# One decode kernel's loads re-planned: 3 MB slots at fixed places, more of the cache kept on chip, program order on every engine

**Chip, cores, metric.** One core of one Trainium2 chip. The metric is device time in microseconds (us), median of several executions; a profile of one execution gives the span, some 1 to 2 us shorter than the time.

## The reference

One token goes twice through attention over a window of 4,096 cached positions and a gated FFN. Cut to what matters:

```python
x = x + _A_ref(_layernorm(x), A_k_cache, A_v_cache, A_wq, A_wo)   # 32 heads, Dh 192, last 4096 positions
x = x + _B_ref(_layernorm(x), B_w1, B_w3, B_w2)                   # D 640, F 1536
x = x + _A_ref(_layernorm(x), A_k_cache, A_v_cache, A_wq, A_wo)   # the same caches and weights again
x = x + _B_ref(_layernorm(x), B_w1, B_w3, B_w2)
```

Every byte of K, V and the weights is used for one token only, so the work is reading: a head's K or V is 1.57 MB, 64 of them a layer. What layer 1 still finds on chip from layer 0 it need not read. wq and wo are the weights before and after the attention; w1, w3 and w2 are those of the FFN.

## The kernel before

A ring of five 1.5 MB pages serves all loads; K of eleven heads stays in tiles of its own. VectorE (DVE) transposes each K page, TensorE (PE) forms scores and weighted sums.

```python
NRING = 5
RETAIN = (0, 1, 2, 8, 9, 10, 16, 17, 18, 24, 25)
...
def k_page(layer, h, s_ps):
    if layer == 0 or h not in RETAIN:
        x = ...                                # a retained tile or a ring page
        nc.sync.dma_start(out=x[:], in_=A_k_cache[0, h, S0:SK, :].rearrange("(p t) d -> p (t d)", p=P))
        ...                                    # two DVE transposes
    for it in range(6):
        be, par = divmod(it, 2)
        for th in range(2):
            nc.tensor.matmul(s_ps[32 * th:32 * th + 32, :], lhsT=wst[:, hl, it, :],
                             rhs=_ap(x[:], 0, P, 3072 * th + 64 * be + par, [[192, 16], [2, 32]]), ...)
...
for layer in range(2):
    attention(layer)      # wq, K and V of 4 blocks of 8 heads, then all of wo
    layernorm()
    ffn(...)
```

Of the kernel before, what the change touches and what calls it, by code (L numbers as in the profile page):

```python
# [13 lines left out]
PSUM = bass.MemoryType.PSUM  # L14

# [9 lines left out]
PGW = 6144  # L25
# [3 lines left out]
NRING = 5  # L29
RETAIN = (0, 1, 2, 8, 9, 10, 16, 17, 18, 24, 25)  # L30
KSPLIT = 2
# [8 lines left out]
def kernel(  # L40
# [16 lines left out]

    cst = ctx.enter_context(tc.tile_pool(name="cst", bufs=1))
    wrk = ctx.enter_context(tc.tile_pool(name="wrk", bufs=1))
    sml = ctx.enter_context(tc.tile_pool(name="sml", bufs=2))  # L60
    ring = ctx.enter_context(tc.tile_pool(name="ring", bufs=NRING))
    xrp = ctx.enter_context(tc.tile_pool(name="xrp", bufs=1))
    ps_s = ctx.enter_context(tc.tile_pool(name="ps_s", bufs=2, space=PSUM))
    ps_a = ctx.enter_context(tc.tile_pool(name="ps_a", bufs=4, space=PSUM))
    ps_m = ctx.enter_context(tc.tile_pool(name="ps_m", bufs=2, space=PSUM))

    nc.scalar.preload_act_table_set("natural_log_exp_and_others")

    xb = cst.tile([P, NCH], BF16, name="xb")
    nc.sync.dma_start(out=xb[:], in_=A_x[0, 0, :].rearrange("(p c) -> p c", c=NCH))  # L70

    onesD = cst.tile([P, P], F32, name="onesD")
# [9 lines left out]

    sel4 = cst.tile([P, 4], BF16, name="sel4")
    nc.gpsimd.memset(sel4[:], 0.0)
    nc.gpsimd.affine_select(out=sel4[:], in_=sel4[:], compare_op=ALU.not_equal, fill=1.0, base=0,
                            pattern=[[-32, 4]], channel_multiplier=1)
    sel16 = cst.tile([P, 4, 4], BF16, name="sel16")
    nc.gpsimd.memset(sel16[:], 0.0)
    nc.gpsimd.affine_select(out=sel16[:], in_=sel16[:], compare_op=ALU.not_equal, fill=1.0, base=0,
                            pattern=[[-32, 4], [-1, 4]], channel_multiplier=1)  # L90
    selp = cst.tile([P, 2, HB], BF16, name="selp")
    nc.gpsimd.memset(selp[:], 0.0)
    for j in range(4):
        nc.gpsimd.affine_select(out=selp[:], in_=selp[:], compare_op=ALU.not_equal, fill=1.0, base=-(32 * j + 14),
                                pattern=[[-1, 2], [2, HB]], channel_multiplier=1)
    dmask = cst.tile([64, HB], F32, name="dmask")
    nc.gpsimd.memset(dmask[:], 0.0)
    for blk in range(8):
        nc.gpsimd.affine_select(out=dmask[:], in_=dmask[:], compare_op=ALU.not_equal, fill=float(D), base=-(8 * blk + 7),
                                pattern=[[1, HB]], channel_multiplier=1)  # L100
    t0 = cst.tile([64, 32], F32, name="t0")
    nc.gpsimd.memset(t0[:], 0.0)
    tb = cst.tile([64, 32], F32, name="tb")
    nc.gpsimd.memset(tb[:], 0.0)

    wst = cst.tile([P, HB, 6, 32], BF16, name="wst")
    ptm = cst.tile([P, 16 * 144], BF16, name="ptm")
    otd = cst.tile([P, 48], BF16, name="otd")
    otp = cst.tile([P, 8, 32], BF16, name="otp")
    htd = cst.tile([P, 12], BF16, name="htd")  # L110
    htp = cst.tile([P, 8, 32], BF16, name="htp")

    qt_sb = cst.tile([P, 2, 6, 16], BF16, name="qt_sb")
    retained = {}

    def layernorm():
        nc.vector.tensor_tensor(out=xsq[:, 6:6 + NCH], in0=xsq[:, 0:NCH], in1=xsq[:, 0:NCH], op=ALU.mult)
        st_ps = ps_m.tile([P, 12], F32, tag="m", name="st_ps")
        nc.tensor.matmul(st_ps[:], lhsT=onesD[:], rhs=xsq[:], start=True, stop=True)
# [13 lines left out]
    def y_to_residual(y_ps, dst=None):  # L133
        y_sb = wrk.tile([P, D], BF16, tag="w20", name="y_sb")
        nc.scalar.copy(out=y_sb[:, 0:320], in_=y_ps[0][:, 0:320])
        nc.vector.tensor_copy(out=y_sb[:, 320:640], in_=y_ps[1][:, 0:320])  # L136
        yt_ps = ps_m.tile([P, NCH], F32, tag="m", name="yt_ps")
        for c in range(NCH):
            nc.tensor.matmul(yt_ps[:, c:c + 1], lhsT=y_sb[:, c:D:NCH], rhs=onesb[:], start=True, stop=True)
        nc.vector.tensor_tensor(out=(xsq[:, 0:NCH] if dst is None else dst), in0=xsq[:, 0:NCH], in1=yt_ps[:], op=ALU.add)  # L140

    wq_v = A_wq.rearrange("(p c) n -> c p n", c=NCH)

    def qproj():
        q_ps = ps_a.tile([P, 512], F32, tag="a", name="q_ps")
        for c in range(NCH):
            pg = ring.tile([P, PGW], BF16, tag="pg", name="wq_pg")
            nc.sync.dma_start(out=pg[:], in_=wq_v[c])
            for c2 in range(4):
                for j in range(4):  # L150
                    hp = 4 * j + c2
                    nc.tensor.matmul(q_ps[32 * j:32 * j + 32, 0:384], lhsT=xs4[:, c, c2, :],  # L152
                                     rhs=pg[:, 384 * hp:384 * hp + 384],
                                     start=(c == 0 and c2 == 0), stop=(c == NCH - 1 and c2 == 3),
                                     tile_position=(0, 32 * j))
        q_rep = [wrk.tile([P, 6, 4, 32], BF16, tag=("w20", "w21")[par], name=f"q_rep{par}") for par in range(2)]
        for par in range(2):
            src = _ap(q_ps[:], 0, P, par, [[64, 6], [0, 4], [2, 32]])
            if par == 0:
                nc.scalar.copy(out=q_rep[par][:], in_=src)  # L160
            else:
                nc.vector.tensor_copy(out=q_rep[par][:], in_=src)  # L162
        qt_ps = ps_m.tile([P, 2, 6, 16], F32, tag="m", name="qt_ps")
        for hh in range(2):
            for it in range(6):
                be, par = divmod(it, 2)
                nc.tensor.matmul(qt_ps[:, hh, it, :],
                                 lhsT=q_rep[par][:, 3 * hh + be, :, :].rearrange("p a k -> p (a k)"),
                                 rhs=sel16[:].rearrange("p j c -> p (j c)"), start=True, stop=True)
        nc.vector.tensor_copy(out=qt_sb[:], in_=qt_ps[:])  # L170

    def build_w(b):
        for a in range(4):
            dst = _ap(wst[:], 32 * a, 32, 8 * a + 7, [[382, 4], [191, 2], [32, 6]])
            src = _ap(qt_sb[:], 32 * a, 32, 4 * b, [[1, 4], [96, 2], [16, 6]])
            if a % 2 == 1:
                nc.scalar.copy(out=dst, in_=src)  # L177
            else:
                nc.gpsimd.tensor_copy(out=dst, in_=src)  # L179

    def k_page(layer, h, s_ps):
        hl = h % HB
        if layer == 0 or h not in RETAIN:
            if h in RETAIN:
                x = xrp.tile([P, PGW], BF16, tag=f"xr{h}", name=f"xr{h}")
                retained[h] = x
            else:
                x = ring.tile([P, PGW], BF16, tag="pg", name="k_pg")
            nc.sync.dma_start(out=x[:], in_=A_k_cache[0, h, S0:SK, :].rearrange("(p t) d -> p (t d)", p=P))
            w = PGW // KSPLIT  # L190
            for sp in range(KSPLIT):
                nc.vector.transpose(x[:, w * sp:w * (sp + 1)].bitcast(U32), x[:, w * sp:w * (sp + 1)].bitcast(U32))  # L192
        else:
            x = retained[h]
        for it in range(6):
            be, par = divmod(it, 2)
            for th in range(2):
                nc.tensor.matmul(s_ps[32 * th:32 * th + 32, :], lhsT=wst[:, hl, it, :],  # L198
                                 rhs=_ap(x[:], 0, P, 3072 * th + 64 * be + par, [[192, 16], [2, 32]]),
                                 start=(hl == 0 and it == 0), stop=(hl == HB - 1 and it == 5),  # L200
                                 tile_position=(0, 32 * th))

    def softmax_chain(s_ps):
# [3 lines left out]
        r2 = sml.tile([32, 2, HB], F32, tag="r2", name="r2")  # L207
        for th in range(2):
            nc.vector.reduce_max(out=r2[:, th, :], in_=_ap(t1[:], 32 * th, 32, 0, [[1, HB], [8, 4]]), axis=AX.X)
        m8 = sml.tile([32, HB], F32, tag="m8", name="m8")  # L210
        nc.vector.reduce_max(out=m8[:], in_=_ap(r2[:], 0, 32, 0, [[1, HB], [HB, 2]]), axis=AX.X)
        mb = _ap(m8[:], 0, 32, 0, [[0, 4], [1, HB]])
        nc.vector.tensor_scalar_mul(out=tb[0:32, :].rearrange("p (a z) -> p a z", a=4), in0=mb, scalar1=-SCALE)
        nc.scalar.mul(out=tb[32:64, :].rearrange("p (a z) -> p a z", a=4), in_=mb, mul=-SCALE)
        nbt = sml.tile([64, 32], F32, tag="nbt", name="nbt")
        nc.vector.transpose(nbt[:], tb[:])
        e = wrk.tile([64, 512], BF16, tag="w20", name="e")
        l = sml.tile([64, 1], F32, tag="l", name="l")
        nc.scalar.activation(out=e[:], in_=s_ps[0:64, :], func=ACTF.Exp, bias=nbt[:, 0:1], scale=SCALE, accum_out=l[:])  # L219
        et = wrk.tile([64, 512], BF16, tag="w21", name="et")  # L220
        nc.vector.transpose(et[:], e[:])  # L221
        engs = [nc.scalar, nc.vector, nc.scalar, nc.vector, nc.scalar, nc.vector, nc.scalar, nc.scalar]
        for th in range(2):
# [31 lines left out]
    def combine(b, o_ps, rl):  # L255
# [14 lines left out]
        if b == 0:  # L270
            nc.gpsimd.tensor_copy(out=otp[:, 0:4, 0], in_=otd[:, 0:4])
# [85 lines left out]
    def attention(layer):  # L357
# [8 lines left out]
        for k in range(HB):  # L366
            k_page(layer, k, s_ps)
# [51 lines left out]
```

## Time and profile before

| | before |
|---|---|
| time, median of 13 runs | 552.07 us (551.77 to 552.55) |
| span of the profiled run | 550.8 us |
| bytes read | 227.29 MB |
| busy: PE, DVE, ACT | 54%, 41%, 8% of the span |

The page cuts the span into 40 slices: a digit is a busy share in tenths, and a second line gives GB/s. A timeline line has start, duration, engine, source line, operation, operands, count, and in brackets the idle time before it with what ended it. A matmul that waited for a DMA therefore dates a landing, which is the moment at which a transfer's data may be used. The lines are shown in the prediction.

### The profile page before, as it was taken

The numbers are of one execution on the slowest core, as the hardware profiler recorded it, in microseconds if no ns is written. First come the engines' busy times: TensorE is split into PE (matmuls) and PEld (weight loads), VectorE is DVE, ScalarE is ACT, GpSimd is POOL, SyncE is SP. The second block draws the span as 40 slices with busy tenths as digits, with TensorE's granted clock in tenths as the row PEclk, the third lists the DMA queues.
The fourth block names the chain that finished last, engine by engine and source line by source line (L and its number), as shares of the span: only waits on it lengthen the run. The fifth ranks groups of instructions, "written<-read, shape, count | busy, mean of one in ns | idle before, by whom it ended". The sixth has DMA issues, their size and how long they took to land.

```text
span 550.8 us, 5786 instructions
## 1 busy us (share of the span) xinstructions
PE 298.8 (54%) x2448; PEld 124.2 (23%) x2448; DVE 226.5 (41%) x270; ACT 41.9 (8%) x107; POOL 12.2 (2%) x52
## 2 busy tenths in 40 slices
PE   2355555647555556644455386457555765553543
PEld 1111122213222222221222132222222322221221
DVE  2189844374444744420012095444344444420011
ACT  1100200030002000020001002001100300020000
POOL 2000000000000000000000000000000000000000
PEclk9999776576676666565556579776877767565556
DMA  8999999999999999999999999999999999999992
GB/s 342 428 423 427 427 425 427 423 424 424 427 426 426 428 425 426 422 426 418 408 420 427 423 417 428 426 425 426 423 426 427 425 427 425 427 423 419 406 420 94
DMA packets 24618, 227.66 MB, mean 413 GB/s; under 512 B 2704, under 2 KB 2704, under 8 KB 7824
## 3 DMA queue, kind: packets, MB, share of 16 engines
q1 hardware_dynamic: 24592, 227.29, 98.4%
q8 instruction: 19, 0.31, 0.2%
q14 instruction: 7, 0.06, 0.0%
HBM read 227.28 MB, written 0.00 MB: 413 GB/s over the span
## 4 chain that ended last, share of the span: by engine, by line
DMA 73%; PE 16%; DVE 7%; ACT 2%; issue 1%; SPq 0%; DVEq 0%; ACTq 0%
DMA k_pg<-in_A_k_cache_dram 42%; PE s_ps L198 9%; DMA wo_pg<-in_A_wo_dram 9%; DMA v_pg<-in_A_v_cache_dram 8%; DVE k_pg L192 6%; PE o_ps L249 5%; DMA wq_pg<-in_A_wq_dram 5%; DMA fd_pg<-in_B_w_dram 5%; DMA xr<-in_A_k_cache_dram 4%; ACT ptm L229 1%; PE y_ps L292 1%; DVE xr L192 1%; PE q_ps L152 1%; PE y_ps L352 0%; ACT e L219 0%
## 5 line engine op out<-in xcount | busy, mean ns | idle before, releaser
L192 DVE STREAM_TRANSPOSE k_pg<-k_pg 128x1536 uint32<-128x1536 uint32 x84 | 144.2, 1756 | 131.7 <-DMA k_pg<-in_A_k_cache_dram 60.3
L198 PE MATMUL s_ps<-k_pg,wst 128*32 128x512 bf16 x504 | 115.9, 543 | 119.8 <-DVE k_pg L192 119.8
L249 PE MATMUL o_ps<-v_pg,ptm 128*16 128x384 bf16 (+1 forms) x1024 | 133.7, 472 | 28.4 <-DMA v_pg<-in_A_v_cache_dram 23.6
L198 PEld LDWEIGHTS <-wst 128*32 128x32 bf16 x768 | 54.9, 116 | 240.4 <-issue 190.5
L198 PE MATMUL s_ps<-xr,wst 128*32 128x512 bf16 x264 | 53.0, 509 | 26.5 <-DVE xr L192 22.9
L249 PEld LDWEIGHTS <-ptm 128*16 128x16 bf16 (+1 forms) x1024 | 49.9, 109 | 72.6 <-issue 57.8
L192 DVE STREAM_TRANSPOSE xr<-xr 128x1536 uint32<-128x1536 uint32 x22 | 37.7, 1753 | 8.7 <-DMA xr<-in_A_k_cache_dram 8.6
L152 PE MATMUL q_ps<-wq_pg,xs 128*32 128x384 bf16 x160 | 14.7, 518 | 21.4 <-DMA wq_pg<-in_A_wq_dram 20.0
L177 ACT COPY wst<-qt_sb 32x48 bf16<-32x48 bf16 x16 | 6.4, 397 | 237.7 <-PE s_ps L198 233.6
L267 DVE TENSOR_TENSOR otd<-ot_ps,rl 64x12 bf16<-64x12 f32 x16 | 2.9, 184 | 51.0 <-PE ot_ps L262 25.5
L292 PE MATMUL y_ps<-wo_pg,otd 128*1 128x320 bf16 x160 | 15.6, 464 | 14.7 <-DMA wo_pg<-in_A_wo_dram 14.7
L136 DVE CAST y_sb<-y_ps 128x320 bf16<-128x320 f32 x4 | 2.0, 492 | 42.4 <-PE y_ps L292 35.2
L229 ACT COPY ptm<-et 32x128 bf16<-32x128 bf16 x40 | 16.2, 404 | 6.6 <-DVE et L221 6.2
L162 DVE CAST q_rep<-q_ps 128x768 bf16<-128x768 f32 x2 | 1.9, 958 | 35.3 <-ACT q_rep L160 35.3
L257 ACT CAST o_sb<-o_ps 128x384 bf16<-128x384 f32 x8 | 3.8, 478 | 148.3 <-PE o_ps L249 148.3
L179 POOL COPY wst<-qt_sb 32x48 bf16<-32x48 bf16 x16 | 6.2, 385 | 320.6 <-PE s_ps L198 243.6
L204 DVE TENSOR_REDUCE t<-s_ps 64x1 f32<-64x512 f32 x8 | 5.4, 678 | 18.5 <-PE s_ps L198 18.5
L152 PEld LDWEIGHTS <-xs 128*32 128x32 bf16 x160 | 6.2, 130 | 28.7 <-issue 22.3
L292 PEld LDWEIGHTS <-otd 128*1 128x1 bf16 x160 | 6.0, 111 | 23.8 <-issue 19.6
L221 DVE STREAM_TRANSPOSE et<-e 64x512 bf16<-64x512 bf16 x8 | 5.6, 703 | 4.6 <-ACT e L219 4.6
L235 PE MATMUL rl_ps<-ld,onesD 64*128 64x8 f32 x16 | 3.7, 302 | 5.9 <-POOL ld L233 5.9
L231 DVE COPY ptm<-et 32x128 bf16<-32x128 bf16 x24 | 6.2, 260 | 0.5
(79 smaller groups left out, 89.8 us busy)
## 6 DMA issues: line engine op xcount, KB each, us to landing
v_pg<-in_A_v_cache_dram SPq DMA_DIRECT2D x64, 1536.0 KB, 13.4
k_pg<-in_A_k_cache_dram SPq DMA_DIRECT2D x42, 1536.0 KB, 15.2
xr<-in_A_k_cache_dram SPq DMA_DIRECT2D x11, 1536.0 KB, 22.3
wq_pg<-in_A_wq_dram SPq DMA_DIRECT2D x10, 1536.0 KB, 14.0
wo_pg<-in_A_wo_dram SPq DMA_DIRECT2D x10, 1440.0 KB, 16.7
fd_pg<-in_B_w_dram SPq DMA_DIRECT2D x4, 960.0 KB, 12.5
fa_pg<-in_B_w_dram SPq DMA_DIRECT2D x2, 1536.0 KB, 14.3
fb_pg<-in_B_w_dram SPq DMA_DIRECT2D x2, 1536.0 KB, 14.5
```

Of the source, the lines that this page charges most:

```text
L152: nc.tensor.matmul(q_ps[32 * j:32 * j + 32, 0:384], lhsT=xs4[:, c, c2, :], rhs=pg[:, 384 * hp:384 * hp + 384], start=(c == 0 and c2 == 0), ...
L177: nc.scalar.copy(out=dst, in_=src)
L179: nc.gpsimd.tensor_copy(out=dst, in_=src)
L192: nc.vector.transpose(x[:, w * sp:w * (sp + 1)].bitcast(U32), x[:, w * sp:w * (sp + 1)].bitcast(U32))
L198: nc.tensor.matmul(s_ps[32 * th:32 * th + 32, :], lhsT=wst[:, hl, it, :], rhs=_ap(x[:], 0, P, 3072 * th + 64 * be + par, [[192, 16], [2, 3 ...
L204: nc.vector.reduce_max(out=t0[:, 0:1], in_=s_ps[0:64, :], axis=AX.X)
L221: nc.vector.transpose(et[:], e[:])
L229: eng.copy(out=dst, in_=src)
L231: eng.tensor_copy(out=dst, in_=src)
L249: nc.tensor.matmul(o_ps[32 * j:32 * j + mw, 0:384], lhsT=ptm[:, po:po + mw], rhs=vn[:, 384 * u:384 * u + 384], start=(hl == 0 and mq == 0) ...
L257: nc.scalar.copy(out=o_sb[:], in_=o_ps[:, 0:384])
L292: nc.tensor.matmul(y_ps[nh][32 * j:32 * j + mw, 0:320], lhsT=lhsT, rhs=pg[:, 640 * cc + 320 * nh:640 * cc + 320 * nh + 320], start=(ci < 4 ...
```

## The change

The intent: read fewer bytes, in longer rows, and let no part of the chip make the queue of transfers wait. A row, or run, is one contiguous piece of DRAM that goes to one partition. The core of the change, with cuts marked:

```diff
-NRING = 5
-RETAIN = (0, 1, 2, 8, 9, 10, 16, 17, 18, 24, 25)
+SLOT = 64 * DH                 # two heads, 24,576 B per partition
+NSLOT = 7                      # fixed places in one large tile, beside a small ring for weights
+CUT_Q0 = (2, 2, 1)             # how a weight is cut into transfers
 ...
+    ctx.enter_context(tc.manual_schedule(engines={ENG.SP, ENG.PE, ENG.DVE, ENG.Activation, ENG.Pool}))
 ...
+    def need(key):             # issues the planned transfers in order, up to this one
 ...
+            nc.sync.dma_start(out=pg[:, at:at + n], in_=src)
 ...
+    def kv_src(cache, b, z, t0=0, nt=TP):
 ...
+        return bass.AP(cache.tensor, cache.offset + off, [[TP * DH, 64], [SK * DH, 2], [1, nt * DH]])
 ...                            # the plan: every transfer with its place
+                                     rhs=_ap(x, 0, P, 192 * th + 64 * be + par + 2 * h, [[384, 32], [4, 16]]),
 ...
+        order = (0, 1, 2, 3) if layer == 0 else (3, 2, 1, 0)     # layer 1 starts with the retained block
+        for z in range(NZ):
+            if layer == 1 and z < 2:
+                q_rows((range(0, 3), range(3, 5))[z])
+            k_stage(order[0], z, s_ps, z == 0, z == NZ - 1)
 ...                            # wo is read and used block by block, inside the attention loop
+    def ffn_out(layer, xr):    # the last product as a row in one column group; the residual as a row
 ...
+                    nc.tensor.matmul(z_ps[nh][0:1, 0:320], lhsT=otd[:, f:f + 1], rhs=w[:, o:o + 320], ...)
 ...
+        nc.sync.dma_start(out=out[0, :, :], in_=ob)              # one row of 1,280 B
```

## The prediction

In its paragraph on rows, a is an engine's time for a row or run and s that for a transfer, beside the time for the bytes. The time for the bytes (3614 ns for a V page, 3388 for a wo page, 7228 for a slot) is at one rate, which the prediction did not fit. What the traces show of it: the two page times by themselves, with nothing for a transfer, give 3,623 ns for the bytes of a V page (434 GB/s), 8.8 ns a row and 7,316 ns a slot (estimate, from 3.693 and 3.607 us); a slot less a V page, as measured later, is 7.30 - 3.693 = 3.607 us (436 GB/s). The times of the last product, 21.5 to 24.8, and the 3 us of the exposed end are estimates.

> **What bounds the kernel now.** I read the page's slices first, then the shares of the chain that ended last, then the times at which consecutive transfers land, and last the two ends of the span.
>
> ```profile
> DMA  8999999999999999999999999999999999999992
> GB/s 342 428 423 427 427 425 427 423 424 424 427 426 426 428 425 426 422 426 418 408 420 427 423 417 428 426 425 426 423 426 427 425 427 425 427 423 419 406 420 94
> q1 hardware_dynamic: 24592, 227.29, 98.4%
> ```
>
> The 16 DMA engines are busy in every slice but the first and the last. The kernel reads 227.29 MB once and nothing stops the queue in between.
>
> ```profile
> DMA 73%; PE 16%; DVE 7%; ACT 2%; issue 1%; SPq 0%; DVEq 0%; ACTq 0%
> ```
>
> The PE and DVE shares of that chain are buffers coming free while other transfers run, not gaps in the queue. No engine is near a bound: the transposes of K are the largest group outside PE, 144.2 + 37.7 us for 53 heads, 3.4 us a head.
>
> So the time is bytes over rate, plus two ends. The rate is read from matmuls released by consecutive landings, V pages (1536 KB, rows of 12,288 B) and wo pages (1440 KB, runs of 3,840 B):
>
> ```profile
> 495.03 1.46 PE L249 MATMUL o_ps<-v_pg,ptm 128*16 128x384 bf16 x16 [3.41 <-DMA v_pg<-in_A_v_cache_dram]
> ...
> 506.11 1.46 PE L249 MATMUL o_ps<-v_pg,ptm 128*16 128x384 bf16 x16 [2.24 <-DMA v_pg<-in_A_v_cache_dram]
> ```
>
> ```profile
> 513.48 0.73 PE L292 MATMUL y_ps<-wo_pg,otp 128*32 128x320 bf16 x8 [1.03 <-DMA wo_pg<-in_A_wo_dram]
> ...
> 524.30 1.76 PE L292 MATMUL y_ps<-wo_pg,otd 128*1 128x320 bf16 x18 [1.85 <-DMA wo_pg<-in_A_wo_dram]
> ```
>
> Three V pages take 11.08 us, 3.693 each; three wo pages take 10.82, 3.607 each, for 6% fewer bytes. Shorter rows cost. The end:
>
> ```profile
> 543.60 0.43 PE L352 MATMUL y_ps<-fd_pg,htd 128*1 128x320 bf16 x2 [1.59 <-DMA fd_pg<-in_B_w_dram]
> ...
> 544.91 0.49 DVE L136 CAST y_sb<-y_ps 128x320 bf16<-128x320 f32 x1 [3.87 <-PE y_ps L352]
> ...
> 546.10 0.35 SPq L388 DMA_DIRECT2D out_dram<-ob  x1
> ```
>
> The last weight page lands at 543.60 and the span ends at 550.8: 7.2 us, of which 4.7 are the store of the result.
>
> [...] Here the first wq page is issued at 1.17 and lands at 7.62; less 3.69 of data that is 2.76 us. [...] The granted clock here is 0.50 around 500 us and 0.99 just after 539, after two busy microseconds; it comes and goes.
>
> **The change, part by part.** Two heads share one transfer, 3 MB in rows of 24,576 B, into seven fixed slots of one large tile; the program order stands on every engine; wo is read by block of eight heads; layer 1 takes the blocks backwards.
>
> *Bytes.* Layer 1 finds on chip four K slots and two and a half V slots of block 3, 13 head-pages. Before it was 11. Two pages less, 3.15 MB, 2 x 3.693 = 7.4 us.
>
> *Rows.* [...] An engine has 8 rows of a V page: 3614 + 8a + s = 3693 ns. It has 24 runs of a wo page: 3388 + 24a + s = 3607. So a = 8.7 ns, s = 9 ns. A slot then takes 7228 + 70 + 9 = 7307 ns, against 7386 for two pages: 1.1%. All transfers by this rule: before 117 K and V pages 432.1, wq 36.9, wo 38.5, FFN 28.1, sum 535.6 us. After: 56 slots 409.2, three half slots 11.1, wq 18.3 + 18.9 (layer 1 in rows of 6,144 B), five whole wo blocks 23.0, nine cuts 14.3, FFN 28.5, sum 523.2 us. Of the 12.4 gained, 7.4 are bytes and 5.0 rows. That extrapolation is the choice I am least able to check. From first landing (7.62) to last (543.60) the old kernel took 536.0, the rule gives 531.9 without its first page: 4.1 are instruction fetches and dips, and I keep 4.0.
>
> *Start.* wq is issued first and x goes by another queue: the issue moves from 1.17 to about 0.75, 0.4 gained.
>
> *DVE, PE, ACT.* 56 heads are transposed in place of 53, by four pieces per slot, 7.0 us against 7.3 of transfer; behind K and V together that hides. The transposes and copies of the softmax double in width (estimate 7 us per block), but a slot is refilled some six transfers (44 us) later, so they hide too. The PE's work is unchanged in count.
>
> *The layer boundary.* This is where the change can lose. All weights from wo of block 3 to wq of layer 1 go through 33 KB per partition, the equivalent of 10 us of transfer, where before five pages held 18 us. Let 0 be the last byte of the last V half. wo and w1 fill the queue until 9.5. w3 overwrites wo: landing 2.1, 16 matmuls 1.5, combine about 2.1, 16 of the wo matmuls 1.6, issue to data about 0.7: 8.0, slack 1.5. w2 overwrites w1: the wo matmuls end near 8, residual and layernorm 3.55 (529.80 to 533.36 before), 8 matmuls 0.8, issue 0.7: about 13.1 against 14.2. The second half of wq needs w2's matmuls, residual, layernorm and a first wq matmul: about 27 against 28.4. The first K slot of layer 1 needs retained K used up, 8 + 24 matmuls (12 take about 2.6) after the third wq piece: about +8.4 against +8.5. Each just fits; I put the expected stall at 0.5 us, up to 4.
>
> *The end.* After the last V only one wo block and the FFN remain, 19.0 us of transfer where before it was 32. From the last V's landing: matmuls 2.9, combine 2.1, wo 24 x 98 ns = 2.4, residual and layernorm 3.5, w1 1.9; then w3 must land (14.3) and takes 0.4; hidden part 2.2; float32 matmuls for the residual row about 1.5: 18.3. The last product is 24 matmuls in one column group[...]: 21.5 to 24.8. w2 is all there at 19.0. After that landing, then, 2.5 to 5.8, two additions about 0.95, the store 2.6 to 4.1 (one row of 1,280 B in place of 128 of 10 B): 6 to 11, I take 7.6 against 7.2.
>
> *Sum.* Issue 0.75 + 2.76 + 523.2 + 4.0 + stall 0.5 + end 7.6 = 538.8 us of span; times lie 1.5 above the span (552.32 against 550.8): **540.3 us**.
>
> **Rivals.** *The boundary stalls for real.* Four waits have slacks near 1 us by estimated durations, and 0.50 clock or an unseen wait eats that. Against it: piece sizes and order look made for it, and waits partly absorb one another. It would give 543 to 548, within 2%. *Long rows bring nothing*: if the engines cut 24 KB rows up, or HBM gives no more, K and V stay at 3.69 a head: 545, within 2%. The two-point fit speaks against. *The end is exposed*: [...]the serial product adds 3 us: 543. *It is all hidden as intended*, [...]fast store: 537. A real slowdown needs a bound elsewhere, such as DVE transposes blocked behind the softmax so slots return late; with 3.5 us a head against 7.4 of K plus V I see none.
>
> **Range and chances.** Faster by over 2% means below 541.3, and my sum lies 1.0 below that, with a spread of about 3 us, skewed to the slow side. The slot planning looks measured rather than guessed, which I count a little in its favour. Range 536 to 546. Faster 0.58, within 2% 0.40, slower 0.02.
>
> **What would show it.** Right: about 224.1 MB read; consecutive slots landing 7.31 us apart (430 GB/s); DMA at 9 in all middle slices, none of the boundary slices below 410; last weight landing to the end of the span 6 to 11 us; DVE busy about 8 us more in transposes. Wrong: slot spacing of 7.39 or more refutes the row step; a slice near the middle below 400 GB/s, or queue waits on PE there of several us with idle engines, refutes the boundary step; more than 11 us after the last landing refutes the end; retained pages still read again refutes the bytes.

## The result and the profile after

The changed kernel takes 538.10 us (median of 8 runs, 537.46 to 538.86) against 552.07: ratio 0.9746, 95% interval 0.9737 to 0.9756, faster by more than 2%. Ratios are the mean time of one kernel's runs over that of the other's of the same rounds, so not quite the ratio of the medians. On the three later chips the kernel before read 0.8 to 1.2 us lower, and on two of them the changed one about 0.3 us lower, so experiments are set against a control, the changed kernel run again: 537.83 and 537.74 on those two chips, 538 in round numbers. The chip of the first four runs (rows in the changed kernel, bytes, the step of K) had no control; from the kernel before there, 550.98 us, and the controls' ratios the changed kernel would take 537.8 on it (estimate).

Slices and queue of the kernel after, from its page:

```profile
DMA  8999999999999999999999999999999999999995
GB/s 354 438 434 425 429 435 426 423 438 431 423 436 421 431 434 434 423 432 432 415 414 409 409 368 427 421 424 437 427 430 428 430 434 429 425 436 428 424 408 222
q1 hardware_dynamic: 14978, 224.14, 98.5%
```

3.15 MB less is read, and the K and V slices are at some 430 GB/s where they were at 425. One slice, the 24th, dips to 368.

Matmuls released by the last three V slots, from the timeline of the kernel after:

```profile
498.35 2.74 PE L337 MATMUL o_ps<-pg,ptm 128*16 128x384 bf16 x32 [3.97 <-DMA pg<-in_A_v_cache_dram]
505.65 2.74 PE L337 MATMUL o_ps<-pg,ptm 128*16 128x384 bf16 x32 [4.56 <-DMA pg<-in_A_v_cache_dram]
512.95 2.74 PE L337 MATMUL o_ps<-pg,ptm 128*16 128x384 bf16 x32 [4.57 <-DMA pg<-in_A_v_cache_dram]
```

Slots land 7.30 us apart, two heads in place of 2 x 3.693 = 7.386; the prediction had 7.307.

The dip, first from the timeline, then from the stretches of one microsecond (columns: stretch, its length, busy time and count of PE, weight load, DVE, ACT and POOL, granted clock, DMA share, GB/s):

```profile
306.15 0.83 PE L254 MATMUL qh_ps<-pg,xs 128*32 128x384 bf16 x8 [1.03 <-DMA pg<-in_A_wq_dram]
306.70 0.33 SPq L98 DMA_DIRECT2D pg<-in_A_wo_dram  x1
306.75 4.70 PE L293 MATMUL s_ps<-pg,wst 128*32 128x512 bf16 x20
...
312.39 6.53 SPq L98 DMA_DIRECT2D pg<-in_A_k_cache_dram  x2
```

```profile
311.00:312.00 1.00, 1.00 (x12) 0.30 (x8) 0.00 (x0) 0.00 (x0) 0.00 (x0) 1.00 0.94 389
312.00:313.00 1.00, 1.00 (x16) 0.73 (x12) 0.00 (x0) 0.00 (x0) 0.00 (x0) 1.00 0.29 118
313.00:314.00 1.00, 1.00 (x7) 0.32 (x4) 0.00 (x0) 0.56 (x1) 0.00 (x0) 1.00 1.35 366
314.00:315.00 1.00, 1.00 (x7) 0.33 (x5) 0.72 (x1) 0.24 (x1) 0.00 (x0) 1.00 0.29 98
```

The third wq piece lands, then 24 matmuls use up the first retained K slot, and only then, at 312.39, may the first K of layer 1 be issued into that slot. The queue is running dry by then, and the first bytes of that K slot come some 1.3 us after the issue:

```profile
313.40:313.60 0.20, 0.20 (x3) 0.00 (x0) 0.00 (x0) 0.16 (x1) 0.00 (x0) 1.00 0.12 51
313.60:313.80 0.20, 0.20 (x4) 0.15 (x2) 0.00 (x0) 0.20 (x1) 0.00 (x0) 1.00 3.16 911
```

Against 425 GB/s the three stretches from 312 to 315 lack 693 KB, 1.6 us. The PE is at 100% there; it is the PE that the queue waits for, and then the way from issue to data.

The end, from the timeline:

```profile
528.52 1.28 PE L436 MATMUL r_ps<-pg,xsq 128*1 128x64 f32 x20
...
529.59 0.19 DVE L418 TENSOR_TENSOR otd<-gut,ex 128x12 bf16<-128x12 f32 x1
...
529.83 3.42 PE L450 MATMUL z_ps<-pg,otd 128*1 128x320 bf16 x24
533.21 0.98 DVE L455 TENSOR_TENSOR pg<-z_ps,pg 1x320 bf16<-1x320 f32 x2 [3.43 <-PE z_ps L450]
534.22 0.32 SPq L457 DMA_DIRECT2D out_dram<-pg  x1
```

The residual row's float32 matmuls lie beside the silu chain and delay nothing: the product starts 0.05 us after its operand is written. It takes 0.142 us a matmul, and the store ends the span at 536.3, 2.1 us after its issue where the old one took 4.7.

### The profile page after: what moved, and what is told of

Its sections match the earlier page's. It is cut to its first block, busy times and chain, and to the rows that moved or that the text cites.

```text
span 536.3 us, 5554 instructions
## 1 busy us (share of the span) xinstructions
PE 282.5 (53%) x2407; PEld 104.9 (20%) x2407; DVE 251.7 (47%) x297; ACT 41.1 (8%) x94; POOL 8.6 (2%) x37
## 3 DMA queue, kind: packets, MB, share of 16 engines
q1 hardware_dynamic: 14978, 224.14, 98.5%
## 4 chain that ended last, share of the span: by engine, by line
DMA 67%; DVE 15%; PE 13%; issue 2%; ACT 1%; SPq 1%; ACTq 0%; DVEq 0%
DMA pg<-in_A_k_cache_dram 52%; DVE pg L286 11%; PE s_ps L293 9%; DMA pg<-in_B_w_dram 5%; DMA pg<-in_A_wo_dram 4%; DMA pg<-in_A_v_cache_dram 3%; PE o_ps L337 2%; DMA pg<-in_A_wq_dram 2%; ACT e L312 1%; DVE et L316 1%; PE y_ps L373 1%; PE z_ps L450 1%; SPq L98 1%; PE qh_ps L254 1%; DVE wst L278 1%
## 5 line engine op out<-in xcount | busy, mean ns | idle before, releaser
L293 PE MATMUL s_ps<-pg,wst 128*32 128x512 bf16 x768 | 175.3, 619 | 158.2 <-DVE pg L286 156.4
L286 DVE STREAM_TRANSPOSE pg<-pg 128x1536 uint32<-128x1536 uint32 x112 | 189.0, 1745 | 105.9 <-DMA pg<-in_A_k_cache_dram 105.8
L337 PE MATMUL o_ps<-pg,ptm 128*16 128x384 bf16 (+1 forms) x1024 | 82.2, 378 | 25.4 <-DMA pg<-in_A_v_cache_dram 24.8
L337 PEld LDWEIGHTS <-ptm 128*16 128x16 bf16 (+1 forms) x1024 | 33.1, 99 | 62.9 <-issue 50.8
L312 ACT ACTIVATE e<-s_ps,nbt 32x512 bf16<-32x512 f32 x16 | 13.1, 821 | 361.2 <-DVE nbt L308 361.0
L373 PE MATMUL y_ps<-pg,otd 128*1 128x320 bf16 x192 | 14.6, 462 | 9.8 <-DVE otd L361 9.2
L316 DVE STREAM_TRANSPOSE et<-e 64x1024 bf16<-64x1024 bf16 x8 | 9.9, 1236 | 15.2 <-ACT e L312 15.2
L325 ACT COPY ptm<-et 32x256 bf16<-32x256 bf16 x32 | 13.5, 421 | 8.0 <-DVE et L316 7.4
L398 PE MATMUL gu_ps<-pg,xs 128*32 128x384 bf16 x80 | 8.2, 501 | 5.7 <-DMA pg<-in_B_w_dram 2.9
L327 DVE COPY ptm<-et 32x256 bf16<-32x256 bf16 x32 | 9.2, 286 | 0.6
```

The source lines that it names most:

```text
L286: nc.vector.transpose(v, v)
L293: nc.tensor.matmul(s_ps[32 * h:32 * h + 32, :], lhsT=wst[:, z, h, it, 4 - 4 * th:36 - 4 * th], rhs=_ap(x, 0, P, 192 * th + 64 * be + par + ...
L312: nc.scalar.activation(out=_ap(e[:], 32 * h, 32, h, [[32, 32], [2, 16]]), in_=s_ps[r, :].rearrange("p (t j) -> p t j", j=16), func=ACTF.Ex ...
L316: nc.vector.transpose(et[:], e[:])
L325: nc.scalar.copy(out=dst, in_=src)
L327: nc.vector.tensor_copy(out=dst, in_=src)
```

## The experiments

Twelve runs, two of them the control. All passed the check of the result, even the one whose scores are wrong: the check does not see that error, so a pass says little about the scores.

**Rows in the changed kernel.** Each slot in two or four transfers along its rows, nothing else:

```diff
-            nc.sync.dma_start(out=pg[:, at:at + n], in_=src)
+            for i, part in enumerate(src ...):        # two (or four) sources of 12,288 (or 6,144) B rows
+                nc.sync.dma_start(out=pg[:, at + m * i:at + m * (i + 1)], in_=part)
```

> The changed kernel with each slot read by two transfers of 12,288 B rows in place of one of 24,576 B; same bytes, slots and order. Theory (a fixed cost per row and per transfer, 8.7 and 9 ns per engine): 56 slots x 79 ns = +4.4 us on 538.1, so 542.5. Rival (row length above 12 KB brings nothing, the gain beyond the bytes came from deeper prefetch and order): 538.1 within 0.5.

> The same with four transfers of 6,144 B rows per slot. Theory: 56 x 237 ns = +13.3 us, so 551.3, which is the time before with 3 MB fewer bytes. Rival: 538.1, or a jump out of line with the step of the run with two transfers, if the number of transfers in flight is the limit.

Measured 543.03 and 552.05 us (ratios 0.9852 and 1.0021): 5.0 and 14.0 above 538 where 4.4 and 13.3 were expected. The landings agree more closely still. V transfers from the timeline of the run with two, then of that with four:

```profile
495.60 0.83 PE L341 MATMUL o_ps<-pg,ptm 128*16 128x384 bf16 x16 [1.26 <-DMA pg<-in_A_v_cache_dram]
...
517.76 1.46 PE L341 MATMUL o_ps<-pg,ptm 128*16 128x384 bf16 x16 [2.24 <-DMA pg<-in_A_v_cache_dram]
```

```profile
499.57 0.82 PE L341 MATMUL o_ps<-pg,ptm 128*16 128x384 bf16 x8 [0.19 <-DMA pg<-in_A_v_cache_dram]
...
524.06 0.82 PE L341 MATMUL o_ps<-pg,ptm 128*16 128x384 bf16 x8 [1.06 <-DMA pg<-in_A_v_cache_dram]
```

Six transfers in 22.16 us are 3.693 each, thirteen in 24.49 are 1.884; the rule gives 3.693 and 1.886. With 6,144 B rows the whole gain is gone although 3.15 MB fewer are read (19 runs, from 550.87 to 554.11, a wider spread than in the other runs). These two cut rows and add transfers at once; the next pair takes them apart. A row of 24,576 B goes as one packet: the page of the run with two transfers counts 23,042 packets on q1 against 14,978, and the 8,064 more are 56 x 128 rows and 56 x 16 packets under 512 B, one for each added transfer and engine.

**Rows in the kernel before.** Each page of K and V in two transfers of 6,144 B rows; or in one transfer of two such runs per row, by letting partition p hold 16 tokens of each half of the window, alike for K and V:

```diff
-nc.sync.dma_start(out=vn[:], in_=A_v_cache[0, h, S0:SK, :].rearrange("(p t) d -> p (t d)", p=P))
+nc.sync.dma_start(out=vn[:].rearrange("p (r x) -> p r x", r=2),
+                  in_=A_v_cache[0, h, S0:SK, :].rearrange("(r p t) d -> p r (t d)", r=2, p=P))
```

> The kernel before, with each K and V page in two transfers of 6,144 B rows. Theory (8.7 ns per row and 9 ns per transfer and engine): 117 pages x 78.8 ns = +9.2 us, 560. Rival (the cost found in the changed kernel is one of its slots, order or depth, and not of rows): no change.

> The kernel before, with each K and V page in one transfer of two runs of 6,144 B per row; tokens are taken in another order, alike for K and V, which leaves the result alone. Theory (runs cost 8.7 ns, a transfer 9): 117 x 69.6 ns = +8.1 us, 559, that is 1.1 below the run with two transfers. Rival (the number of transfers costs, not that of runs): no change.

Measured 560.47 and 559.86 us against 551.26 for the kernel before on the same chip (ratios 1.0166 and 1.0157): +9.2 and +8.6, expected +9.2 and +8.1. One transfer with two runs costs nearly as much as two transfers. So it is runs that cost, and the rule holds in the other kernel too. The intervals (about 0.3% wide) do not resolve the 9 ns per transfer, and the landings show none of it. V from the timeline of the run with two transfers, then of that with two runs in one:

```profile
501.67 0.82 PE L253 MATMUL o_ps<-v_pg,ptm 128*16 128x384 bf16 x8 [1.99 <-DMA v_pg<-in_A_v_cache_dram]
...
518.61 0.82 PE L253 MATMUL o_ps<-v_pg,ptm 128*16 128x384 bf16 x8 [1.07 <-DMA v_pg<-in_A_v_cache_dram]
```

```profile
503.30 1.46 PE L251 MATMUL o_ps<-v_pg,ptm 128*16 128x384 bf16 x16 [3.48 <-DMA v_pg<-in_A_v_cache_dram]
...
518.37 1.46 PE L251 MATMUL o_ps<-v_pg,ptm 128*16 128x384 bf16 x16 [2.32 <-DMA v_pg<-in_A_v_cache_dram]
```

Nine half pages in 16.94 us are 3.76 us a page, four pages in 15.07 are 3.77: the second transfer of a page costs nothing that can be seen, its shorter runs 0.07 to 0.08 us.

**Bytes.** One retained V slot read again in layer 1:

```diff
     plan_k(1, 2, 1, 3)
+    plan_v(1, 3, 1, 6)
 ...
-                keys = [("v", 0 if (b == 3 and z in (1, 2)) else layer, b, z)]
+                keys = [("v", 0 if (b == 3 and z == 2) else layer, b, z)]
```

> The changed kernel, but one of the retained V slots of block 3 (two heads, 3.15 MB) is read again in layer 1, after the second K slot. Theory (the time is bytes over rate): +7.3 us, 545.4. Rival (part of the read hides in the pause at the layer boundary, or the boundary is bound by compute): +5.7 or less.

Measured 545.45 us (ratio 0.9900), 7.5 above 538. Two head-pages are worth their transfer time (7.3 us expected), and nothing of it hides.

**The pause at the layer boundary.** Two runs. In the first the K matmuls read at the old step between columns, which gives wrong scores:

```diff
-  rhs=_ap(x, 0, P, 192 * th + 64 * be + par + 2 * h, [[384, 32], [4, 16]]),
+  rhs=_ap(x, 0, P, 192 * th + 64 * be + par + 2 * h, [[384, 32], [2, 16]]),
```

> Wrong result on purpose: the matmuls of K read their columns at a step of 4 B as before in place of 8 B, same counts. Theory (the 8 B step slows the matmul at full clock, 0.22 us against 0.14 us each): the mean of the K matmuls falls from 619 to about 540 ns. On the path it can only shorten the wait of the first K slot of layer 1: 0.5 to 1.2 us off, 537.0 to 537.6. Rival (the matmuls are slow for another reason, such as the two column groups): mean stays near 619 ns, 538.1.

The K matmuls as a group (count, busy us, mean ns), in the kernel after and in this run. Then the 24 matmuls of one slot, as stretches of line 293 alone (length, busy time and count of PE and of weight load, granted clock, DMA share, GB/s): two slots of the kernel after, at full clock and near half, and two of this run, likewise:

```profile
L293 PE MATMUL s_ps<-pg,wst 128*32 128x512 bf16 x768 | 175.3, 619 | 158.2 <-DVE pg L286 156.4
```

```profile
L293 PE MATMUL s_ps<-pg,wst 128*32 128x512 bf16 x768 | 151.5, 549 | 179.4 <-DVE pg L286 171.9
```

```profile
59.05:64.60 5.55, 5.55 (x24) 1.27 (x23) 1.00 1.01 434
144.00:149.40 5.40, 5.39 (x24) 1.43 (x23) 0.51 0.98 419
```

```profile
44.28:47.93 3.65, 3.65 (x24) 1.82 (x24) 1.00 1.00 431
193.50:198.80 5.30, 5.30 (x24) 1.89 (x23) 0.50 1.00 425
```

The step of 8 B, which comes from interleaving two heads over the partitions, costs the PE a third of its speed at full clock: 5.55 us for 24 matmuls against 3.65, 0.23 against 0.15 us each. Near half clock it costs next to nothing, 5.39 against 5.30: with this step the PE gains nothing from its full clock. The matmuls ran in pairs in two column groups; one alone was not tried. Much of both runs passes at half clock (mean granted clock 0.752 and 0.728), so the mean fell by 11% only. 24 us of PE time less bought what was expected and little more: the first K slot of layer 1 was issued at 311.07 in place of 312.39, and the span fell from 536.3 to 534.9. The time, 537.12 us, is some 0.7 us below the estimate for its chip; this run has no control on its chip, so its ratio (0.9748) alone does not settle it.

The second keeps the result right. The third wq row goes between the two halves of the slot's matmuls, so that they start as soon as their weights are ready:

```diff
         for th in range(2):
+            if th == 1 and between is not None:
+                between()                                  # the third wq row
 ...
-                q_rows((range(0, 3), range(3, 5))[z])
+                q_rows((range(0, 2), range(3, 5))[z])
```

> The changed kernel with one row of wq in layer 1 taken between the two halves of the first retained K slot's matmuls in place of ahead of them, so that the slot comes free about 1 us earlier and the piece of wo behind that wq row is still issued in time. Theory (the pause of the queue there is the PE's wait, 1.6 us): -0.8 to -1.5 us from the control, and no slice of 1 us under 300 GB/s there. Rival (the pause is a transfer's start-up or some other wait): no change.

Measured 537.05 us against the control's 537.83 (ratios 0.9757 and 0.9763; their intervals overlap, because one of its four runs read 539.01; the other three lie at 536.8 to 537.1). The K slot was issued at 310.91, and the stretches of this run show the pause gone:

```profile
312.00:313.00 1.00, 1.00 (x7) 0.55 (x5) 0.21 (x1) 0.76 (x1) 0.00 (x0) 1.00 1.59 463
313.00:314.00 1.00, 1.00 (x8) 0.48 (x6) 0.74 (x1) 0.00 (x0) 0.00 (x0) 1.00 0.56 238
314.00:315.00 1.00, 1.00 (x7) 0.55 (x5) 0.00 (x0) 0.00 (x0) 0.00 (x0) 1.00 1.28 541
```

One stretch is still under 300, which the expectation had excluded, but the three together carry 414 GB/s where they carried 194. The queue did wait for the PE.

**The end.** The old end in the changed kernel, then the last product in two column groups with two stores:

```diff
-            ffn_out(layer, residual_row())
+            ffn_down_out(layer)        # four column groups, column sums turned to partitions, 128 x 10 B stored
```

```diff
-  nc.tensor.matmul(z_ps[nh][0:1, 0:320], lhsT=otd[:, f:f + 1], rhs=w[:, o:o + 320], ...)
+  nc.tensor.matmul(z_ps[nh][32 * nh:32 * nh + 1, 0:320], ..., tile_position=(0, 32 * nh))
```

> The changed kernel with the old end: the last product in four column groups, the column sums turned by matmuls to 128 partitions, and the result stored as 128 pieces of 10 B. Theory (the serial product costs 1.7 us more but saves the turning and a slow store, 4.7 us against 2.1): +1.0 to +2.3 us over the control. Rival (the serial product is the loss): -1 us.

> The changed kernel with the two halves of the last product side by side in two column groups, and two stores. The product is then 24 matmuls in about 1.8 us in place of 3.4. Theory (the end is a chain of compute, but the last w2 piece lands only some 1 us before the product's end): -0.4 to -1.2 us. Rival (the last landing bounds the end): 0.

The old end took 539.13 us, +1.3 on the control. Its product was not done much earlier, because its last matmuls had to wait for w2; the turning and the store then took 5.0 us against 3.1 for the additions and the new store. From its timeline:

```profile
531.43 1.47 PE L373 MATMUL y_ps<-pg,otd 128*1 128x320 bf16 x12 [0.30 <-DMA pg<-in_B_w_dram]
532.94 0.43 ACT L380 CAST y_sb<-y_ps 128x320 bf16<-128x320 f32 x1 [3.77 <-PE y_ps L373]
...
534.17 0.34 SPq L435 DMA_DIRECT2D out_dram<-ob  x1
```

That run's span ends at 537.9. Two column groups took 537.13 us, 0.7 below the control:

```profile
529.67 0.98 PE L449 MATMUL z_ps<-pg,otd 128*1 128x320 bf16 x12
530.88 1.19 PE L449 MATMUL z_ps<-pg,otd 128*1 128x320 bf16 x12 [0.23 <-DMA pg<-in_B_w_dram]
```

Here the product waits for w2 at 530.88. It ends at 532.07 where the serial one ended at 533.25, so the serial product cost about 1.2 us. The medians show 0.7 of it and the profiled spans 0.9 (535.3 against the control's 536.2); two additions and two stores then take 3.3 us there, where the end before took 3.1.

**All together.** Both repairs, and wo of the last block in one transfer; beside it the second control (the first stood beside the runs of the end and the boundary):

> The changed kernel itself again, as the control for this chip, since the ratio to the kernel before may shift a little from chip to chip (the first four runs all came out 0.2 to 0.3% slower than expected against it). Ratio 0.974 to 0.977.

> The changed kernel once more, as the control for this call's chip: 537.5 to 538.5.

> The two repairs together (the wq row between the halves of the first retained K slot, and the last product in two column groups), and wo of the last block in one transfer. Their gains add up if one is in the pause of the queue and the other after the last byte: -0.8 and -0.7 and -0.2 from the control, 536.1 to 536.5. If the end is bound by the last landing, the second half of that gain is lost: 537.

535.90 us (535.68 to 536.46) against 537.74 (ratios to the kernel before 0.9724 and 0.9757): the gains add, as they should with one in the queue's pause and the other after the last byte. The intervals of the two ratios do not meet (0.9709 to 0.9738, 0.9741 to 0.9774), which the boundary run alone could not show, and the stretches from 312 to 315 carry 398, 390 and 418 GB/s. What wo in one transfer adds was not run apart. This is the fastest version, faster than both kernels.

## Why the prediction was right, and what in it was off

It said 540.3 us, 536 to 546, faster with 0.58; the run gave 538.1, so 12.0 us of gain predicted (from 552.32, the median of the four runs that it had) and 14.0 measured. Bytes and rows, 12.4 us, were right in cause and size. The terms around them were not, and it is partly luck that they missed in opposite directions: with its own end of 7.6 us the time would have been 541.0, just inside the 541.3 that it needed.

- *Bytes* (7.4 us): right. 224.14 MB were read, and reading one slot again cost 7.5 us.
- *Rows* (5.0 us over all transfers, 4.4 of them on K and V against 12,288 B): right, and confirmed in the step it was least sure of. Slots landed 7.30 us apart; with 3.693 and 1.884 us for a half and a quarter of the bytes that is 1.2% between rows of 12 and 24 KB and 2.0% between 6 and 12. The cost per run was shown in both kernels, at three row lengths in one and two in the other. Of its two costs the one per transfer, 9 ns, was not borne out.
- *Start* (0.4 us): right. The first slot of wq landed at 10.68 us; the sum had 0.75 + 2.76 + 7.31 = 10.8. x, 1.2 KB from ACT beside rows of 24,576 B from SP, took 6.2 us to land; in the kernel before, alone ahead of the first page, it took 1.7.
- *DVE, PE and ACT hide*: right for the time, with one thing missed. The K transposes grew by 7.1 us in all (189.0 against 181.9) and hid. But "the PE's work is unchanged in count" overlooked that each K matmul became slower at full clock, which mattered in one place: without it the slot there was issued 1.3 us earlier.
- *The layer boundary* (0.5 us of stall): this term was too small, though within the "up to 4" given. By its own test, a middle slice under 400 GB/s, it failed: the slice read 368 (two neighbours, rich in short weight rows, 409) and the pause was 1.6 us. Of the four slacks, the last fell short. Its compute was about right: with 2.6 us for 12 K matmuls it had 5.2 for 24, and these ended 5.4 us after the wq row, at an issue 6.2 us after that row began (8 matmuls and 24, 6.0 by its terms). What failed is the comparison: landing 2.1 (an estimate: the 2.76 of the first page less 0.7), 8 matmuls 0.8 and 24 at 5.2 make 8.1 of its +8.4, which leaves 0.3 us from issue to data, where two of the other waits were given 0.7 and the trace shows 1.3. The other three waits show no gap: the stretch from 260 to 310 kept a DMA share of 1.01.
- *The end* (7.6 us after the last landing): too large. The last w2 piece landed at about 531.6 (estimate, from the last matmuls of the run with two column groups; good to a few tenths), so the end is about 4.7 us, below the 6 given as the least. Three parts were mis-sized: 1.5 us for the float32 matmuls of the residual row, which ran beside the silu chain; the array, which was at full clock (granted 1.00 from 529 us on), 0.142 us a matmul, where the middle of the range was 0.2 (21.5 to 24.8 less 18.3, over 24); and the store of one row, 2.1 us in place of 2.6 to 4.1. The 128 pieces of 10 B ended 4.7 us after their issue in the kernel before and 3.7 in the run with the old end.

These account for the miss of 2.5 us in the span: +1.1 from the pause, -2.9 from the end, and -0.7 that remain, not measured apart, for the allowance of 4.0 for fetches (0.31 MB on q8, 0.2% of the engines' time, on both pages) and dips and for the start. What the fixed program order on every engine is worth was not tested apart either: bytes, rows, start and end less the pause (7.4 + 5.0 + 0.4 + 2.5 - 1.6) make 13.7 of the 14.5 us by which the span fell, so little is left for it. No rival was needed; the serious one, a boundary that stalls for several microseconds, was there at a third of that size.

Rate and clock, as the traces have them: slots that land 7.30 us apart are 431 GB/s. The slices of the kernel before read 428 at most; five of the slices of 13.4 us of the kernel after read 436 to 438, while over 40 us the highest that was read there is 434 (20 to 60 us), so whether the slices show a higher rate or only how packets are counted stays open. At the end, from 524 to 528 us, the PE was 78 to 100% busy in each microsecond at a granted clock of 0.50; in the next the clock was 0.92, and 1.00 from 529 on. Why it rose there was not tested.

## What to carry to other kernels

Where a kernel only streams, count bytes and runs: fit a time per byte and a time per run from two transfers of different row length in its own trace, and the worth of longer rows can be told before anything is built, here (434 GB/s and 8.8 ns a run on each engine) to about a tenth of a percent of the time. What was left here lay at the two ends and in one place where a buffer was freed late (a pause of 1.6 us); find such places by listing, for each refill, the compute between the landing it needs and the issue, add the way from issue to data, and compare the sum with what the queue still holds. A faster engine was worth nothing elsewhere here: 24 us of PE time bought about one.
